# Decode attention over a long cache: larger K and V chunks, softmax by quarter heads, and a deeper add tree for the scores

## The chip, the cores and the metric

The kernel runs on one core of a Trainium2 chip. The metric is device time in microseconds from the first to the last instruction of the core. A core has a matrix engine (TensorE, PE in the profile), a vector engine (VectorE, DVE), an engine for activation functions (ScalarE, ACT), a general one (GpSimd, POOL) and one that mostly issues transfers (SyncE, SP). Data come from the off-chip memory into the on-chip SBUF, 128 partitions wide, through 16 DMA engines that all issuing engines share.

## The reference

One token is decoded. A single row `x` of 512 numbers goes through two branches, mixed by a scalar gate:

```
q = x @ wq                                  # 32 heads of 128
scores[h, k] = q[h] . K[h, k] / sqrt(128)    # K cache: 32 x 65536 x 128, bf16
o[h] = softmax(scores[h]) @ V[h]             # V cache: the same shape
a = o @ wo
b = (silu(x @ w_gate) * (x @ w_up)) @ w_down # hidden width 1792
g = sigmoid(sum(x * gate_w))
out = g * a + (1 - g) * b
```

The two caches are 537 MB each, and every byte is used once. All weights together are about 14 MB.

## The kernel before, in words

The start loads `x`, the gate's row and all weights (`wq_sb`, `wo_sb`, `wg_sb`, `wu_sb`, `wd_sb`), each whole, into one pool that stays open. TensorE makes q, already copied to all 128 partitions (`X_bc` holds x copied along columns, L67 and L85), ScalarE puts it into `q_bc_sb` (L92). The FFN branch gives `b_sb` (L96 to L134), the gate gives `gval`.

Then comes the stream, a loop over 32 heads. For each head, 16 chunks of 4096 keys are loaded, a chunk being a tile `K_t` of 128 partitions x 32 keys x 128 numbers, 1 MB, 8 KB a partition. The scores come from VectorE, not from TensorE: it multiplies the tile by q, repeated for each of the 32 keys (L175), and sums the 128 products of a key. Two adds fold them from 128 to 64 (L176) and to 32 (L180), in place; a reduce sums the last 32 (L184) into 32 columns of the head's score tile `S_sb`.

When the 512 columns of a head are there, ScalarE takes the exponential of all of them in one instruction (L189), which also leaves the sum of each row in `rowsum`. No maximum is subtracted. The result `P_sb` goes to TensorE: for each of the 16 chunks of V (`V_t`, 1 MB), 32 matmuls with 128 x 128 of V as the weights and one column of `P_sb` as the moving data, all added up in column h of `O_ps` (L203).

After the last head, the row sums are added over the partitions (L212), `O_ps` is divided by them (L214, L216), `wo` is applied (L220) and the two branches are mixed (L229, L231).

K is loaded through SP's queue, V through ACT's. There are three buffers for K, three for V, two for the products (`prod`), two for `S_sb` and two for `P_sb`. The order of the instructions on each engine isn't the order of the source: the framework picks it when it builds the program, among what it takes to be ready, and adds all waits. In the trace, for instance, the four VectorE operations of two neighbouring chunks are interleaved, and the first three V loads of a head stand ahead of its exponential. An engine carries out its own list strictly in order, so an instruction or a load that waits holds up all that stands behind it on its engine.

Of the kernel before, what the change touches and what calls it, by code (L numbers as in the profile page):

```python
# [7 lines left out]
ACT = mybir.ActivationFunctionType  # L8
ALU = mybir.AluOpType
AXIS = mybir.AxisListType  # L10
P = 128


@with_exitstack
def kernel(
# [14 lines left out]
    nc = tc.nc  # L30
    bf16 = mybir.dt.bfloat16
    f32 = mybir.dt.float32

    _, H, Sk, Dh = A_k_cache.shape
    D = A_x.shape[2]
    F = B_w_gate.shape[1]
    KT = D // P
    FT = F // P
    assert Dh == P
    W = min(4096, Sk)  # L40
    assert Sk % W == 0
    NCH = Sk // W
    J = W // P
    NB = Sk // P
    assert NB <= 512
    assert H % 4 == 0
    scale = float(Dh) ** -0.5

    consts = ctx.enter_context(tc.tile_pool(name="consts", bufs=1))
    wpool = ctx.enter_context(tc.tile_pool(name="weights", bufs=1))  # L50
    psum_q = ctx.enter_context(tc.tile_pool(name="psum_q", bufs=2, space=bass.MemoryType.PSUM))
    psum_o = ctx.enter_context(tc.tile_pool(name="psum_o", bufs=1, space=bass.MemoryType.PSUM))
    psum_misc = ctx.enter_context(tc.tile_pool(name="psum_misc", bufs=2, space=bass.MemoryType.PSUM))

    ones = consts.tile([P, P], f32, name="ones")
    nc.gpsimd.memset(ones, 1.0)

    xT = consts.tile([P, KT], bf16, name="xT")
    nc.sync.dma_start(out=xT, in_=A_x[0, 0, :].rearrange("(t p) -> p t", p=P))
    x_row = consts.tile([1, D], bf16, name="x_row")  # L60
    nc.sync.dma_start(out=x_row, in_=A_x[0])
    gw_row = consts.tile([1, D], bf16, name="gw_row")
    nc.sync.dma_start(out=gw_row, in_=gate_w.unsqueeze(0))

    X_bc = consts.tile([P, KT, P], bf16, name="X_bc")
    for t in range(KT):
        nc.vector.tensor_copy(out=X_bc[:, t, :], in_=xT[:, t : t + 1].to_broadcast([P, P]))  # L67

    wq_sb = wpool.tile([P, KT, H * Dh], bf16, name="wq_sb")
    nc.sync.dma_start(out=wq_sb, in_=A_wq.rearrange("(t p) f -> p t f", p=P))  # L70
    wo_sb = wpool.tile([P, H, D], bf16, name="wo_sb")
    nc.gpsimd.dma_start(out=wo_sb, in_=A_wo.rearrange("(h p) n -> p h n", p=P))
    wg_sb = wpool.tile([P, KT, F], bf16, name="wg_sb")
    nc.scalar.dma_start(out=wg_sb, in_=B_w_gate.rearrange("(t p) f -> p t f", p=P))
    wu_sb = wpool.tile([P, KT, F], bf16, name="wu_sb")
    nc.scalar.dma_start(out=wu_sb, in_=B_w_up.rearrange("(t p) f -> p t f", p=P))
    wd_sb = wpool.tile([P, FT, D], bf16, name="wd_sb")
    nc.gpsimd.dma_start(out=wd_sb, in_=B_w_down.rearrange("(t p) n -> p t n", p=P))

    q_bc_sb = consts.tile([P, H * Dh], bf16, name="q_bc_sb")  # L80
    HG = 4
    for g in range(H // HG):
        qg_ps = psum_q.tile([P, HG * Dh], f32, name="qg_ps")
        for t in range(KT):
            nc.tensor.matmul(  # L85
                qg_ps,
                lhsT=X_bc[:, t, :],
                rhs=wq_sb[:, t, g * HG * Dh : (g + 1) * HG * Dh],
                start=(t == 0),
                stop=(t == KT - 1),  # L90
            )
        nc.scalar.activation(  # L92
            out=q_bc_sb[:, g * HG * Dh : (g + 1) * HG * Dh], in_=qg_ps, func=ACT.Copy
        )

    gu_ps = psum_misc.tile([P, 2 * FT], f32, name="gu_ps", tag="misc")  # L96
    for ft in range(FT):
        for t in range(KT):
            nc.tensor.matmul(  # L99
                gu_ps[:, ft : ft + 1],  # L100
                lhsT=wg_sb[:, t, ft * P : (ft + 1) * P],
                rhs=xT[:, t : t + 1],
                start=(t == 0),
                stop=(t == KT - 1),
            )
        for t in range(KT):
            nc.tensor.matmul(  # L107
                gu_ps[:, FT + ft : FT + ft + 1],
                lhsT=wu_sb[:, t, ft * P : (ft + 1) * P],
                rhs=xT[:, t : t + 1],  # L110
                start=(t == 0),
                stop=(t == KT - 1),
            )
    gu_sb = consts.tile([P, 2 * FT], f32, name="gu_sb")
    nc.vector.tensor_copy(out=gu_sb, in_=gu_ps)  # L115
    eg = consts.tile([P, FT], f32, name="eg")
    nc.scalar.activation(out=eg, in_=gu_sb[:, :FT], func=ACT.Exp, scale=-1.0)
    nc.vector.tensor_scalar_add(eg, eg, 1.0)
    nc.vector.reciprocal(eg, eg)
    hprod = consts.tile([P, FT], f32, name="hprod")  # L120
    nc.vector.tensor_tensor(out=hprod, in0=gu_sb[:, :FT], in1=eg, op=ALU.mult)
    hT = consts.tile([P, FT], bf16, name="hT")
    nc.vector.tensor_tensor(out=hT, in0=hprod, in1=gu_sb[:, FT:], op=ALU.mult)
    b_ps = psum_misc.tile([1, D], f32, name="b_ps", tag="misc")
    for ft in range(FT):
        nc.tensor.matmul(  # L126
            b_ps,
            lhsT=hT[:, ft : ft + 1],
            rhs=wd_sb[:, ft, :],
            start=(ft == 0),  # L130
            stop=(ft == FT - 1),
        )
    b_sb = consts.tile([1, D], f32, name="b_sb")
    nc.vector.tensor_copy(out=b_sb, in_=b_ps)  # L134

    xg = consts.tile([1, D], f32, name="xg")
    s_t = consts.tile([1, 1], f32, name="s_t")
    nc.vector.tensor_tensor_reduce(
        out=xg, in0=x_row, in1=gw_row, scale=1.0, scalar=0.0,
        op0=ALU.mult, op1=ALU.add, accum_out=s_t,  # L140
    )
    eg2 = consts.tile([1, 1], f32, name="eg2")
    nc.scalar.activation(out=eg2, in_=s_t, func=ACT.Exp, scale=-1.0)
    nc.vector.tensor_scalar_add(eg2, eg2, 1.0)
    gval = consts.tile([1, 1], f32, name="gval")
    nc.vector.reciprocal(gval, eg2)

    kpool = ctx.enter_context(tc.tile_pool(name="kt", bufs=3))
    vpool = ctx.enter_context(tc.tile_pool(name="vt", bufs=3))
    prodpool = ctx.enter_context(tc.tile_pool(name="prod", bufs=2))  # L150
    spool = ctx.enter_context(tc.tile_pool(name="s_sb", bufs=2))
    ppool = ctx.enter_context(tc.tile_pool(name="p_sb", bufs=2))

    rowsum = consts.tile([P, H], f32, name="rowsum")
    nc.vector.memset(rowsum, 0.0)
    O_ps = psum_o.tile([P, H], f32, name="O_ps")

    for h in range(H):
        S_sb = spool.tile([P, NB], f32, name="S_sb")
        qb = q_bc_sb[:, h * Dh : (h + 1) * Dh]  # L160
        q_rep = bass.AP(
            tensor=qb.tensor,
            offset=qb.offset,
            ap=[list(qb.ap[0]), [0, J], [1, Dh]],
        )
        for c in range(NCH):
            K_t = kpool.tile([P, J, Dh], bf16, name="K_t")
            nc.sync.dma_start(
                out=K_t,
                in_=A_k_cache[0, h, c * W : (c + 1) * W, :].rearrange(  # L170
                    "(p j) d -> p j d", j=J
                ),
            )
            prod = prodpool.tile([P, J, Dh], bf16, name="prod")
            nc.vector.tensor_tensor(out=prod, in0=K_t, in1=q_rep, op=ALU.mult)  # L175
            nc.vector.tensor_tensor(  # L176
                out=prod[:, :, 0:64], in0=prod[:, :, 0:64], in1=prod[:, :, 64:128],
                op=ALU.add,
            )
            nc.vector.tensor_tensor(  # L180
                out=prod[:, :, 0:32], in0=prod[:, :, 0:32], in1=prod[:, :, 32:64],
                op=ALU.add,
            )
            nc.vector.tensor_reduce(  # L184
                out=S_sb[:, c * J : (c + 1) * J], in_=prod[:, :, 0:32],
                axis=AXIS.X, op=ALU.add,
            )
        P_sb = ppool.tile([P, NB], bf16, name="P_sb")
        nc.scalar.activation(  # L189
            out=P_sb, in_=S_sb, func=ACT.Exp, scale=scale,  # L190
            accum_out=rowsum[:, h : h + 1],
        )
        for c in range(NCH):
            V_t = vpool.tile([P, J, Dh], bf16, name="V_t")
            nc.scalar.dma_start(
                out=V_t,
                in_=A_v_cache[0, h, c * W : (c + 1) * W, :].rearrange(
                    "(p j) d -> p j d", j=J
                ),
            )  # L200
            for j in range(J):
                col = c * J + j
                nc.tensor.matmul(  # L203
                    O_ps[:, h : h + 1],
                    lhsT=V_t[:, j, :],
                    rhs=P_sb[:, col : col + 1],
                    start=(col == 0),
                    stop=(col == NB - 1),
                )

    tot_ps = psum_misc.tile([P, H], f32, name="tot_ps", tag="misc")
    nc.tensor.matmul(tot_ps, lhsT=ones, rhs=rowsum, start=True, stop=True)  # L212
    recip = consts.tile([P, H], f32, name="recip")
    nc.vector.reciprocal(out=recip, in_=tot_ps)  # L214
    oT = consts.tile([P, H], bf16, name="oT")
    nc.vector.tensor_tensor(out=oT, in0=O_ps, in1=recip, op=ALU.mult)  # L216

# [1 line left out]
    for h in range(H):  # L219
# [4 lines left out]
            start=(h == 0),  # L224
# [41 lines left out]
```

The softmax here doesn't subtract the row's maximum and nothing guards it: scores larger than these inputs give would overflow.

## Time and profile before

| | before |
|---|---|
| time, median of 4 runs | 2842.59 us (2840.87 to 2846.31) |
| span of the profiled run | 2842.2 us |
| VectorE busy | 2604.9 us, 92% |
| TensorE matmul / ScalarE busy | 535.7 us, 19% / 29.6 us, 1% |
| moved by DMA | 1090.12 MB, mean 384 GB/s |
| K_t, V_t: from issue to landing | 11.0 us, 13.8 us (median) |

The profile's page lists busy times by engine, the span in 40 slices (each digit the busy share in tenths), and the groups of instructions by source line. A row of a group reads: line, engine, operation, what is written and read with its shape, the count; then total busy time and the mean of one in ns; then how long the engine stood idle just before these instructions and what ended that. The time from issue to landing of a transfer has the transfers ahead of it in it. Rows of busy time by stretch list busy time and count of PE, PE's weight loads, DVE, ACT and POOL, then the granted clock of TensorE, the share of time that the 16 DMA engines were busy, and GB/s.

### The profile page before, as it was taken

The page shows a single profiled execution, that of the slowest core. Times are in us where ns is not written, and L with a number is a line of the kernel's source. Part 1 is how long each engine was busy: PE and PEld are TensorE (multiplying, and loading weights), DVE is VectorE, ACT ScalarE, POOL GpSimd, SP SyncE. Part 2 cuts the span into 40 slices and gives each one's busy share as a digit, 9 for nine tenths or more (in the row PEclk, how much of TensorE's full clock was granted, in tenths as well). Part 3 has the DMA queues.
Part 4 walks back from the last instruction along what each step waited for, and adds up shares of the span by engine and source line. Part 5 has one row for each costly group of instructions (what it writes and reads, how often), then busy time and mean ns, then how long its engine had stood idle before and what let it go on. Part 6 is the DMA issues. An engine that isn't in the chain of part 4 may idle for free.

```text
span 2842.2 us, 37968 instructions
## 1 busy us (share of the span) xinstructions
PE 535.7 (19%) x16576; PEld 485.7 (17%) x16576; DVE 2604.9 (92%) x2067; ACT 29.6 (1%) x75; POOL 3.3 (0%) x7
## 2 busy tenths in 40 slices
PE   2021111121111121111121111121111121111123
PEld 1021111121111121111121111121111121111122
DVE  1999999999999999999999999999999999999992
ACT  0000000000000000000000000000000000000000
POOL 0000000000000000000000000000000000000000
PEclk8555555555555555555555555555555555555555
DMA  8599999999999999999999999999999999999996
GB/s 314 198 393 388 390 390 389 416 394 391 389 390 389 415 395 387 386 389 390 416 394 391 389 387 388 416 395 387 391 388 390 415 394 390 389 389 389 417 395 235
DMA packets 151244, 1090.12 MB, mean 384 GB/s; under 512 B 16995, under 2 KB 16998, under 8 KB 19494
## 3 DMA queue, kind: packets, MB, share of 16 engines
q1 hardware_dynamic: 74790, 541.10, 46.4%
q10 hardware_dynamic: 74784, 540.57, 46.3%
q0 software_dynamic: 1504, 6.03, 0.5%
q8 instruction: 129, 2.11, 0.3%
q14 instruction: 37, 0.30, 0.0%
HBM read 1087.64 MB, written 0.00 MB: 383 GB/s over the span
## 4 chain that ended last, share of the span: by engine, by line
DVE 62%; DMA 26%; issue 10%; PE 2%; another core or an unknown queue 1%; ACT 0%; DVEq 0%; ACTq 0%; SPq 0%
DVE prod L175 30%; DMA K_t<-in_A_k_cache_dram 17%; DVE prod L176 17%; DVE prod L180 8%; DVE S_sb L184 7%; DMA V_t<-in_A_v_cache_dram 7%; DMA wu_sb<-in_B_w_up_dram 1%; PE O_ps L203 1%; PE qg_ps L85 0%; PE a_ps L220 0%; PE b_ps L126 0%; PE gu_ps L107 0%; ACT P_sb L189 0%; PE gu_ps L99 0%
## 5 line engine op out<-in xcount | busy, mean ns | idle before, releaser
L175 DVE TENSOR_TENSOR prod<-K_t,q_bc_sb 128x4096 bf16<-128x4096 bf16 x512 | 1154.4, 2286 | 125.4 <-DMA K_t<-in_A_k_cache_dram 123.6
L203 PE MATMUL O_ps<-P_sb,V_t 128*128 128x1 bf16 x16384 | 507.7, 166 | 2249.5 <-DMA V_t<-in_A_v_cache_dram 1535.0
L203 PEld LDWEIGHTS <-V_t 128*128 128x128 bf16 x16384 | 474.2, 104 | 2283.5 <-DMA V_t<-in_A_v_cache_dram 1694.3
L176 DVE TENSOR_TENSOR prod<-prod 128x2048 bf16<-128x2048 bf16 x512 | 603.1, 1220 | 0.0
L184 DVE TENSOR_REDUCE S_sb<-prod 128x32 f32<-128x1024 bf16 x512 | 599.3, 1213 | 0.0
L180 DVE TENSOR_TENSOR prod<-prod 128x1024 bf16<-128x1024 bf16 x512 | 330.0, 687 | 0.0
L189 ACT ACTIVATE P_sb<-S_sb 128x512 bf16<-128x512 f32 x32 | 20.2, 630 | 2693.3 <-DVE S_sb L184 1763.9
L216 DVE TENSOR_TENSOR oT<-O_ps,recip 128x32 bf16<-128x32 f32 x1 | 0.2, 192 | 37.7 <-PE O_ps L203 37.7
L115 DVE COPY gu_sb<-gu_ps 128x28 f32<-128x28 f32 x1 | 0.2, 186 | 31.0 <-PE gu_ps L107 31.0
L134 DVE COPY b_sb<-b_ps 1x512 f32<-1x512 f32 x1 | 0.7, 679 | 20.8 <-PE b_ps L126 20.8
L85 PE MATMUL qg_ps<-wq_sb,X_bc 128*128 128x512 bf16 x32 | 10.2, 491 | 0.0
L126 PE MATMUL b_ps<-wd_sb,hT 128*1 128x512 bf16 x14 | 5.7, 573 | 16.8 <-DMA wd_sb<-in_B_w_down_dram 16.8
L220 PE MATMUL a_ps<-wo_sb,oT 128*1 128x512 bf16 x32 | 8.6, 436 | 0.3 <-DVE oT L216 0.3
L229 DVE TENSOR_TENSOR diff<-a_ps,b_sb 1x512 f32<-1x512 f32 x1 | 0.7, 679 | 8.7 <-PE a_ps L220 8.7
L107 PE MATMUL gu_ps<-xT,wu_sb 128*128 128x1 bf16 x56 | 3.0, 165 | 20.1 <-DMA wu_sb<-in_B_w_up_dram 20.1
L99 PE MATMUL gu_ps<-xT,wg_sb 128*128 128x1 bf16 x56 | 3.1, 165 | 16.3 <-DMA wg_sb<-in_B_w_gate_dram 16.3
L67 DVE COPY X_bc<-xT 128x128 bf16<-128x128 bf16 x4 | 0.6, 222 | 5.9 <-DMA xT<-in_A_x_dram 5.9
L107 PEld LDWEIGHTS <-wu_sb 128*128 128x128 bf16 x56 | 2.6, 104 | 20.2 <-DMA wu_sb<-in_B_w_up_dram 20.2
L189 ACT ACTIVATION_READ_ACCUMULATOR P_sb<-S_sb 128x1 f32 x32 | 6.0, 187 | 0.0
L99 PEld LDWEIGHTS <-wg_sb 128*128 128x128 bf16 x56 | 2.6, 104 | 16.3 <-DMA wg_sb<-in_B_w_gate_dram 16.3
L92 ACT ACTIVATE q_bc_sb<-qg_ps 128x512 bf16<-128x512 f32 x8 | 4.8, 597 | 27.1 <-PE qg_ps L85 27.1
L126 PEld LDWEIGHTS <-hT 128*1 128x1 bf16 x14 | 1.5, 110 | 20.5 <-issue 20.4
(25 smaller groups left out, 15.9 us busy)
## 6 DMA issues: line engine op xcount, KB each, us to landing
K_t<-in_A_k_cache_dram SPq DMA_DIRECT2D x512, 1024.0 KB, 11.0
V_t<-in_A_v_cache_dram ACTq DMA_DIRECT2D x512, 1024.0 KB, 13.8
wo_sb<-in_A_wo_dram POOLq DMA_DIRECT2D x1, 4096.0 KB, 49.6
wq_sb<-in_A_wq_dram SPq DMA_DIRECT2D x1, 4096.0 KB, 26.0
wg_sb<-in_B_w_gate_dram ACTq DMA_DIRECT2D x1, 1792.0 KB, 15.5
wu_sb<-in_B_w_up_dram ACTq DMA_DIRECT2D x1, 1792.0 KB, 35.4
wd_sb<-in_B_w_down_dram POOLq DMA_DIRECT2D x1, 1792.0 KB, 59.2
xT<-in_A_x_dram SPq DMA_DIRECT2D x1, 1.0 KB, 6.1
```

What stands on the lines that cost most here:

```text
L85: nc.tensor.matmul(qg_ps, lhsT=X_bc[:, t, :], rhs=wq_sb[:, t, g * HG * Dh : (g + 1) * HG * Dh], start=(t == 0), stop=(t == KT - 1),)
L92: nc.scalar.activation(out=q_bc_sb[:, g * HG * Dh : (g + 1) * HG * Dh], in_=qg_ps, func=ACT.Copy)
L99: nc.tensor.matmul(gu_ps[:, ft : ft + 1], lhsT=wg_sb[:, t, ft * P : (ft + 1) * P], rhs=xT[:, t : t + 1], start=(t == 0), stop=(t == KT - 1),)
L107: nc.tensor.matmul(gu_ps[:, FT + ft : FT + ft + 1], lhsT=wu_sb[:, t, ft * P : (ft + 1) * P], rhs=xT[:, t : t + 1], start=(t == 0), stop=(t ...
L126: nc.tensor.matmul(b_ps, lhsT=hT[:, ft : ft + 1], rhs=wd_sb[:, ft, :], start=(ft == 0), stop=(ft == FT - 1),)
L175: nc.vector.tensor_tensor(out=prod, in0=K_t, in1=q_rep, op=ALU.mult)
L176: nc.vector.tensor_tensor(out=prod[:, :, 0:64], in0=prod[:, :, 0:64], in1=prod[:, :, 64:128], op=ALU.add,)
L180: nc.vector.tensor_tensor(out=prod[:, :, 0:32], in0=prod[:, :, 0:32], in1=prod[:, :, 32:64], op=ALU.add,)
L184: nc.vector.tensor_reduce(out=S_sb[:, c * J : (c + 1) * J], in_=prod[:, :, 0:32], axis=AXIS.X, op=ALU.add,)
L189: nc.scalar.activation(out=P_sb, in_=S_sb, func=ACT.Exp, scale=scale, accum_out=rowsum[:, h : h + 1],)
L203: nc.tensor.matmul(O_ps[:, h : h + 1], lhsT=V_t[:, j, :], rhs=P_sb[:, col : col + 1], start=(col == 0), stop=(col == NB - 1),)
L220: nc.tensor.matmul(a_ps, lhsT=oT[:, h : h + 1], rhs=wo_sb[:, h, :], start=(h == 0), stop=(h == H - 1),)
```

## The change

The change touches the stream and the start. Its aims are to give VectorE less to do for each key, to let V follow K more closely, and to get q sooner.

- A chunk is 8192 keys: tiles of 2 MB, 16 KB a partition, three for K (`KT_BUFS`) and four for V (`VT_BUFS`). VectorE works on a chunk in two halves, each as large as a chunk of before.
- In each half the add tree goes on: 128 to 64, 32, 16 and 8 by adds; the reduce sums only the last 8.
- The softmax is taken by segments of two chunks (`CHUNKS_PER_SEG` is 2), a quarter of a head: `S_sb` and `P_sb` have 128 columns and three buffers each, `rowsum` has a column for each segment, and a small reduce (`tot_h`) adds the four of a head at the end.
- At the start, `wq` is loaded in four parts on two queues, in a pool that is closed once q is made; the FFN weights are in a pool that is closed once `b_sb` and the gate are made. The K and V pools are opened after that. The load of `wo` is made to wait for q, by a one-column write into its tile.

The core of the diff:

```diff
-    W = min(4096, Sk)
+    W = min(8192, Sk)
     J = W // P
+    JH = J // 2
...
+    CPS = min(CHUNKS_PER_SEG, NCH)
+    NSEG = NCH // CPS
+    SEGCOLS = CPS * J
...
-    wq_sb = wpool.tile([P, KT, H * Dh], bf16, name="wq_sb")
-    nc.sync.dma_start(out=wq_sb, in_=A_wq.rearrange("(t p) f -> p t f", p=P))
-    nc.gpsimd.dma_start(out=wo_sb, in_=A_wo.rearrange("(h p) n -> p h n", p=P))
...
+    with tc.tile_pool(name="wq_pool", bufs=1) as wq_pool, tc.tile_pool(
+        name="psum_q", bufs=2, space=bass.MemoryType.PSUM
+    ) as psum_q:
+        wq_sb = wq_pool.tile([P, KT, H * Dh], bf16, name="wq_sb")
+        FQ = H * Dh // 4
+        for i in range(4):
+            (nc.sync if i % 2 == 0 else nc.scalar).dma_start(
+                out=wq_sb[:, :, i * FQ : (i + 1) * FQ], in_=wq_v[:, :, i * FQ : (i + 1) * FQ]
+            )
...
+    with tc.tile_pool(name="ffn_w", bufs=1) as wpool:
+        nc.gpsimd.dma_start(out=wg_sb, in_=B_w_gate.rearrange("(t p) f -> p t f", p=P))
+        nc.sync.dma_start(out=wu_sb, in_=B_w_up.rearrange("(t p) f -> p t f", p=P))
+        nc.sync.dma_start(out=wd_sb, in_=B_w_down.rearrange("(t p) n -> p t n", p=P))
+        nc.gpsimd.tensor_copy(out=wo_sb[:, 0, 0:1], in_=q_bc_sb[:, H * Dh - 1 : H * Dh])
+        nc.gpsimd.dma_start(out=wo_sb, in_=A_wo.rearrange("(h p) n -> p h n", p=P))
...
-    kpool = ctx.enter_context(tc.tile_pool(name="kt", bufs=3))
-    vpool = ctx.enter_context(tc.tile_pool(name="vt", bufs=3))
+    kpool = ctx.enter_context(tc.tile_pool(name="kt", bufs=KT_BUFS))
+    vpool = ctx.enter_context(tc.tile_pool(name="vt", bufs=VT_BUFS))
...
-            nc.vector.tensor_tensor(out=prod, in0=K_t, in1=q_rep, op=ALU.mult)
-            nc.vector.tensor_tensor(
-                out=prod[:, :, 0:64], in0=prod[:, :, 0:64], in1=prod[:, :, 64:128],
-                op=ALU.add,
-            )
-            nc.vector.tensor_tensor(
-                out=prod[:, :, 0:32], in0=prod[:, :, 0:32], in1=prod[:, :, 32:64],
-                op=ALU.add,
-            )
-            nc.vector.tensor_reduce(
-                out=S_sb[:, c * J : (c + 1) * J], in_=prod[:, :, 0:32],
-                axis=AXIS.X, op=ALU.add,
-            )
+                for u in range(2):
+                    prod = prodpool.tile([P, JH, Dh], bf16, name="prod")
+                    nc.vector.tensor_tensor(
+                        out=prod, in0=K_t[:, u * JH : (u + 1) * JH, :], in1=q_rep, op=ALU.mult
+                    )
+                    half = Dh
+                    while half > 8:
+                        half //= 2
+                        nc.vector.tensor_tensor(
+                            out=prod[:, :, 0:half], in0=prod[:, :, 0:half],
+                            in1=prod[:, :, half : 2 * half], op=ALU.add,
+                        )
+                    nc.vector.tensor_reduce(
+                        out=S_sb[:, ci * J + u * JH : ci * J + (u + 1) * JH], in_=prod[:, :, 0:8],
+                        axis=AXIS.X, op=ALU.add,
+                    )
```

For each segment of a head, after its chunks of K, the exponential of its 128 columns follows, then the two chunks of V with 64 matmuls each, adding to the same column of `O_ps` over the whole head.

## The prediction

> **What bounds the kernel now.** I read first the page's busy shares and its 40 slices, to see which resources are near full.
>
> ```profile
> PE 535.7 (19%) x16576; PEld 485.7 (17%) x16576; DVE 2604.9 (92%) x2067; ACT 29.6 (1%) x75; POOL 3.3 (0%) x7
> DVE  1999999999999999999999999999999999999992
> DMA  8599999999999999999999999999999999999996
> ```
>
> Two are nearly full at once: VectorE at 92% and the DMA engines in the nines. TensorE and ScalarE are far from any limit. The three lower digits of the DMA row matter too: slice 2 and the last are low, so there is a start and an end in which the transfers don't run full.
>
> Second, the groups by line, for what VectorE does and what it waits for:
>
> ```profile
> L175 DVE TENSOR_TENSOR prod<-K_t,q_bc_sb 128x4096 bf16<-128x4096 bf16 x512 | 1154.4, 2286 | 125.4 <-DMA K_t<-in_A_k_cache_dram 123.6
> L176 DVE TENSOR_TENSOR prod<-prod 128x2048 bf16<-128x2048 bf16 x512 | 603.1, 1220 | 0.0
> L184 DVE TENSOR_REDUCE S_sb<-prod 128x32 f32<-128x1024 bf16 x512 | 599.3, 1213 | 0.0
> L180 DVE TENSOR_TENSOR prod<-prod 128x1024 bf16<-128x1024 bf16 x512 | 330.0, 687 | 0.0
> ```
>
> All but a few us of VectorE is these four; it waits 123.6 us for K, nowhere else in the stream. Third, the timeline of VectorE in the steady part:
>
> ```profile
> 1027.26 4.49 DVE L175 TENSOR_TENSOR prod<-K_t,q_bc_sb 128x4096 bf16<-128x4096 bf16 x2
> 1031.66 2.36 DVE L176 TENSOR_TENSOR prod<-prod 128x2048 bf16<-128x2048 bf16 x2
> 1033.93 1.29 DVE L180 TENSOR_TENSOR prod<-prod 128x1024 bf16<-128x1024 bf16 x2
> 1035.14 2.34 DVE L184 TENSOR_REDUCE S_sb<-prod 128x32 f32<-128x1024 bf16 x2
> 1037.39 4.49 DVE L175 TENSOR_TENSOR prod<-K_t,q_bc_sb 128x4096 bf16<-128x4096 bf16 x2
> ```
>
> Two chunks go side by side: each operation is issued for the one, then for the other. A pair takes 1037.39 - 1027.26 = 10.13 us, so 5.065 us for 4096 keys, although the four durations sum to 2286 + 1220 + 687 + 1213 = 5406 ns: successive instructions overlap by 341/4 = 85 ns each. A head is 8 pairs, 81.0 us.
>
> Fourth, busy time by stretch, for what the DMA does inside a head:
>
> ```profile
> 1008.00:1072.00 64.00, 12.15 (x384) 11.28 (x385) 59.67 (x48) 0.00 (x0) 0.00 (x0) 0.50 1.01 422
> 1072.00:1088.00 16.00, 2.70 (x96) 2.61 (x95) 16.00 (x13) 0.72 (x2) 0.00 (x0) 0.50 0.72 267
> 68.00:147.00 79.00, 5.44 (x68) 2.91 (x67) 74.85 (x60) 3.11 (x6) 0.00 (x0) 0.54 0.48 186
> 147.10:232.30 85.20, 15.77 (x514) 14.72 (x512) 81.13 (x65) 0.72 (x2) 0.00 (x0) 0.50 0.96 395
> 2788.00:2830.00 42.00, 16.33 (x514) 15.13 (x513) 0.55 (x2) 0.46 (x2) 0.00 (x0) 0.50 0.84 326
> ```
>
> The last two columns are DMA share and GB/s. While V and K both stream, the DMA is saturated at 422 GB/s (first row); then the three V buffers are full, V must wait for the softmax of the whole head, and the rate falls to 267 (second). So a head is 85.2 us at 395 GB/s: 81.1 of VectorE and 4 of waiting for K in the saturated part. In the first head V can't run at all (186 GB/s, 79 us), and after the last K chunk V of the last head still has to come (42 us with VectorE idle). The waits confirm that end:
>
> ```profile
> DVE prod L175 <- DMA K_t<-in_A_k_cache_dram: 123.6, 51, 4.2
> DVE oT L216 <- PE O_ps L203: 37.7, 1, 37.7
> ```
>
> The bound today is thus VectorE, with the DMA 2% behind it: 33.55 MB per head at 422 GB/s is 79.5 us.
>
> **What the Trainium skill says.** "VectorE: DVE Perf Modes", The perf-mode tier table: a bf16 tensor_tensor runs two elements a cycle, a tensor_reduce one. The trace agrees: 1024 more output elements cost the add 1220 - 687 = 533 ns (0.52 ns each), and the reduce takes 1213 ns for 1024. The same page, "The DRAIN you can't avoid", has the next operation start only when the pipe is empty; here the trace differs, with 85 ns of overlap when the neighbours are independent. "DMA: Bandwidth & Descriptors", Where 436 GB/s comes from, puts a core's ceiling at 435 GB/s; I see 422. The same page, Issuing engines are not separate DMA queues: loads of SP and ACT share 16 DMA engines; the trace agrees, K and V sharing the 422.
>
> **The change part by part.**
>
> *Deeper tree (half 64, 32, 16, 8; then a reduce over 8).* Multiply and the first two adds keep their sizes, since a half chunk is again 32x128. From 1220 and 687 the add costs 154 + 0.52 n ns, so the one with 512 outputs costs 420 and that with 256 costs 287. The reduce goes from 1024 to 256 elements: at 1.04 ns an element its fixed part is 1213 - 1067 = 146, so 413. Sum per 4096 keys: 2286 + 1220 + 687 + 420 + 287 + 413 = 5313, less 6 x 85 = 4803 ns, against 5065. No trace shows adds with rows of 16 or 8; the rows of 64 and 32 cost the same per element, so I take no penalty. Upper bound: both at one element a cycle, 687 and 420, which gives 5203 ns. Over 512 units: 2459 us (upper 2664) against 2593 before.
>
> *Chunks of 8192 keys.* Loads of 2 MB, half as many. The bytes are the same; both halves of a K tile free it 4.4 us after it is begun. With 3 K and 4 V buffers, 14 MB can be in flight or waiting, against 6.
>
> *Segments of two chunks (128 exp instructions instead of 32).* Exp is between 215 ns (14 columns, L117) and 630 (512), plus 187; ScalarE is 1% busy and this hides. What it moves is V: TensorE may use V after a quarter head, and four V buffers hold two segments. On ACT, the V loads wait for a V buffer and the next exp is queued behind them; but the buffer is freed by TensorE within about 4 us of an exp (32 matmuls take 1.0 us; 128 make 4), and the next exp is 19 us off, so nobody waits for that. In steady state a segment needs 4 x 2.097 MB = 8.39 MB, 19.9 us at 422, while VectorE needs 4 x 4.80 = 19.2. The DMA becomes the bound, and K being always short keeps it full.
>
> *First head and end.* V lags K by a segment and not a head, so the 79 us at 186 GB/s and the 42 us at the end mostly go. At the end after the last K chunk: two units 9.6, exp 0.8, 128 matmuls 4, and what now follows the last V matmul (2829.8 to 2842.2) 12.4: 27 us; 30 with some backlog on VectorE.
>
> *Start.* wq in four loads, wo held until q exists, FFN weights in a pool that is closed before the K pool opens. If K tiles reuse this memory (32 + 42 KB a partition), the first K load waits for the FFN matmuls; behind it on SP are all K loads, and VectorE waits for these. Estimate: wq (4.2 MB, 10 us at 422 GB/s, and about 2 to begin) by 12 us; 32 q matmuls at 0.38 (16 took 6.03 us) to about 26; FFN weights (5.5 MB, 13 us alone, more beside wo and V) to 45; the FFN's matmuls (3 us for the first two products) and the first K tile (2 MB, 5 to 10 us) to 57. Before, the stream began at 42 and stood still from 51 to 72 for b_sb, which is much the same. Meanwhile wo and four V tiles (8.4 MB) can load. I put 15 us of idle DMA here (0 to 35). The four more output columns of tot and tot_h at the end cost below 1 us.
>
> *Sum.* Bytes as before, 1090 MB, at 422 GB/s: 2583 us; first bytes 3; idle at the start 15; end 30: **2631 us**. The other side: VectorE would be through at 57 + 2459 + 17 = 2533, so it waits about 100 us for K.
>
> **Rivals.**
> - *The DMA runs faster with 16 KB rows.* For: half as many descriptors. Against: 422 is already near a share of 1.01, and 435 is the stated ceiling. At 430: 2535 + 48 = 2583 us.
> - *The DMA keeps its gaps* (share 0.96 as in today's heads, for K and V filling together). For: 395 GB/s in each head. Against: today's gap comes from VectorE being slower than the DMA and from the wait of a whole head. 1090/0.405 + 48 = 2739 us.
> - *Short rows run at half rate*, and VectorE stays the bound: 57 + 2664 + 17 = 2738 us.
> - *The halves aren't interleaved.* Then every instruction follows the one it depends on. In the FFN chain at 40.2 us such neighbours have a gap of 0.04 us in place of the overlap: 5313 + 6 x 40 = 5553 ns, 2843 in all, and 57 + 2843 + 17 = 2917 us, slower. For: two halves of one tile are new. Against: two prod buffers, as today, where the order came out interleaved.
>
> **How the numbers follow.** Forecast 0.62; faster DMA 0.10; gaps 0.12; short rows 0.08; no interleaving 0.07; about the same through a mix of losses 0.01. The predicted time is 2631. From 2580 to 2740 takes in the first four, with the ends of start (0 to 35 us) and rate, and leaves out some of the short rows and the slower one. Faster 0.92, same 0.01, slower 0.07.
>
> **What would show it.** Right: DMA at 0.97 or more in nearly every slice at about 420 GB/s; the two new adds near 420 and 287 ns, the reduce near 413; pairs of units at 9.6 us when K is there; a wait for K near 100 us; K wait as the largest item of the chain; oT waiting 6 us or less behind TensorE's last stretch. Wrong: VectorE above 97% busy in the middle (short rows), single instructions with gaps between them (no interleaving), or slices at 390 GB/s with both K and V full.

## The result, and the profile after

The changed kernel takes 2613.55 us (median of 8 runs, 2612.91 to 2615.25). Its ratio to the kernel before is 0.9195, 95% interval [0.9186, 0.9204]. The forecast was 2631 us; it was 17 us too long, for a gain of 229 us where 212 were forecast.

From the page of the changed kernel, the busy shares and the slices:

```profile
PE 482.6 (18%) x16576; PEld 467.1 (18%) x16576; DVE 2485.0 (95%) x3093; ACT 58.1 (2%) x267; POOL 3.2 (0%) x8
DVE  0899999999999999999999999999999999999997
DMA  9999999999999999999999999999999999999995
GB/s 342 370 425 427 427 426 428 427 427 427 427 427 427 427 427 427 428 427 427 427 426 425 425 426 423 427 425 425 427 424 427 424 426 426 425 426 425 424 426 216
```

The same row of the kernel before:

```profile
GB/s 314 198 393 388 390 390 389 416 394 391 389 390 389 415 395 387 386 389 390 416 394 391 389 387 388 416 395 387 391 388 390 415 394 390 389 389 389 417 395 235
```

The GB/s rows decide. In all slices but the first two and the last the rate now stands at 423 to 428, where before it stood at 386 to 417. VectorE's share has risen to 95%, though its work has shrunk: the span has shrunk more. That high share is a trap, and the experiments show it.

The groups of VectorE's stream, different shapes kept apart (mean ns of one after the comma):

```profile
L200 DVE TENSOR_TENSOR prod<-K_t,q_bc_sb 128x4096 bf16<-128x4096 bf16 x512 | 1150.0, 2288 | 45.3 <-DMA K_t<-in_A_k_cache_dram 30.0 <-DVE S_sb L210 0.9
L206 DVE TENSOR_TENSOR prod<-prod 128x2048 bf16<-128x2048 bf16 x512 | 602.7, 1219 | 0.0
L206 DVE TENSOR_TENSOR prod<-prod 128x1024 bf16<-128x1024 bf16 x512 | 329.5, 685 | 0.0
L206 DVE TENSOR_TENSOR prod<-prod 128x512 bf16<-128x512 bf16 x512 | 193.3, 419 | 0.0
L210 DVE TENSOR_REDUCE S_sb<-prod 128x32 f32<-128x256 bf16 x512 | 189.1, 411 | 0.3 <-DVE prod L206 0.3
L206 DVE TENSOR_TENSOR prod<-prod 128x256 bf16<-128x256 bf16 x512 | 124.8, 285 | 0.0
```

The three new sizes cost 419, 285 and 411 ns. The timeline of VectorE at the start of the stream shows how they are strung:

```profile
67.68 0.68 DVE L156 COPY b_sb<-b_ps 1x512 f32<-1x512 f32 x1 [16.31 <-PE b_ps L149]
75.33 4.49 DVE L200 TENSOR_TENSOR prod<-K_t,q_bc_sb 128x4096 bf16<-128x4096 bf16 x2 [6.97 <-DMA K_t<-in_A_k_cache_dram]
79.74 4.63 DVE L206 TENSOR_TENSOR prod<-prod 128x2048 bf16<-128x2048 bf16 x8
84.29 0.74 DVE L210 TENSOR_REDUCE S_sb<-prod 128x32 f32<-128x256 bf16 x2
84.95 4.48 DVE L200 TENSOR_TENSOR prod<-K_t,q_bc_sb 128x4096 bf16<-128x4096 bf16 x2
```

The two halves of a chunk go in step: two multiplies, eight adds, two reduces. Where K is there, a pair takes 84.95 - 75.33 = 9.62 us. Over the whole stream it is slower: the last pair ends at 2592.9 us, and (2592.9 - 75.3)/256 is 9.83 us. The excess is 256 x 0.21 = 55 us in all. The group of the multiply shows 45.3 us of idle time ahead of it; 7.0 of these lie ahead of the first pair, so 38 us belong to the excess, mostly behind K and in gaps of a few tenths of a us. The other 17 us I put down to overlap between neighbours that is lost where a multiply has to wait; no view shows that by itself. With K in plenty (half of V loaded, below) the excess is gone.

Busy time by stretch (the last two columns are DMA share and GB/s) gives the balance of the transfers:

```profile
0.00:90.00 90.00, 18.45 (x158) 8.43 (x159) 18.08 (x30) 6.48 (x11) 3.19 (x8) 0.68 0.88 341
90.00:150.00 60.00, 10.65 (x384) 10.47 (x384) 60.00 (x76) 1.21 (x6) 0.00 (x0) 0.50 0.97 397
900.00:1200.00 300.00, 53.28 (x1920) 53.63 (x1921) 294.22 (x369) 6.14 (x30) 0.00 (x0) 0.50 1.01 427
2560.00:2612.00 52.00, 16.63 (x290) 10.51 (x290) 35.25 (x51) 0.80 (x4) 0.00 (x0) 0.59 0.38 160
```

The page counts 1090.1 MB, which at about 426.5 GB/s, the rate of the stream, are 2556 us. What a stretch moves less than that rate is called lost DMA time here. In the first 90 us 30.7 MB were moved, 72 us worth: 18 us lost. In the next 60, 4 us lost. In the last 52, 8.3 MB or 20 us worth: 32 us lost. The sum, 2556 + 18 + 4 + 32 = 2610 us, is within 2 us of the span of 2611.8. Lost isn't always idle: from 30 to 60 us, while the weights load, the DMA share is 1.03 at only 376 GB/s, and that is 4 of the 18 us.

### The profile page after: what moved, and what is told of

The parts are those of the page before. It is cut to its first block, busy times and chain, and to the rows that moved or that the text cites. A ratio compares the mean times of both kernels' runs of the same rounds, so it can differ in the third digit from the quotient of the medians.

```text
span 2611.8 us, 38109 instructions
## 1 busy us (share of the span) xinstructions
PE 482.6 (18%) x16576; PEld 467.1 (18%) x16576; DVE 2485.0 (95%) x3093; ACT 58.1 (2%) x267; POOL 3.2 (0%) x8
## 2 busy tenths in 40 slices
DMA packets 80189, 1090.10 MB, mean 417 GB/s; under 512 B 8851, under 2 KB 10646, under 8 KB 14486
## 4 chain that ended last, share of the span: by engine, by line
DVE 50%; DMA 48%; PE 1%; issue 1%; DVEq 0%; SPq 0%; ACT 0%; ACTq 0%
DMA K_t<-in_A_k_cache_dram 46%; DVE prod L200 28%; DVE prod L206 20%; DVE S_sb L210 3%; DMA wd_sb<-in_B_w_down_dram 1%; DMA wq_sb<-in_A_wq_dram 1%; PE a_ps L258 0%; PE b_ps L149 0%; PE qg_ps L96 0%; PE O_ps L231 0%; DVEq L200 0%; DVE out_sb L269 0%; DVE diff L267 0%; PE tot_ps L240 0%; SPq L69 0%
## 5 line engine op out<-in xcount | busy, mean ns | idle before, releaser
L200 DVE TENSOR_TENSOR prod<-K_t,q_bc_sb 128x4096 bf16<-128x4096 bf16 x512 | 1150.0, 2288 | 45.3 <-DMA K_t<-in_A_k_cache_dram 30.0
L206 DVE TENSOR_TENSOR prod<-prod 128x2048 bf16<-128x2048 bf16 (+3 forms) x2048 | 1186.0, 652 | 0.0
L231 PE MATMUL O_ps<-P_sb,V_t 128*128 128x1 bf16 x16384 | 454.6, 165 | 2074.8 <-ACT P_sb L215 2074.8
L231 PEld LDWEIGHTS <-V_t 128*128 128x128 bf16 x16384 | 455.4, 104 | 2074.4 <-issue 1688.3
L210 DVE TENSOR_REDUCE S_sb<-prod 128x32 f32<-128x256 bf16 x512 | 189.1, 411 | 0.3 <-DVE prod L206 0.3
L215 ACT ACTIVATE P_sb<-S_sb 128x128 bf16<-128x128 f32 x128 | 39.6, 309 | 2491.4 <-DVE S_sb L210 2412.3
L215 ACT ACTIVATION_READ_ACCUMULATOR P_sb<-S_sb 128x1 f32 x128 | 23.9, 186 | 0.0
L149 PE MATMUL b_ps<-wd_sb,hT 128*1 128x512 bf16 x14 | 5.2, 553 | 12.4 <-DMA wd_sb<-in_B_w_down_dram 12.4
## 6 DMA issues: line engine op xcount, KB each, us to landing
K_t<-in_A_k_cache_dram SPq DMA_DIRECT2D x256, 2048.0 KB, 24.8
```

The lines of the kernel that those rows point to most:

```text
L149: nc.tensor.matmul(b_ps, lhsT=hT[:, ft : ft + 1], rhs=wd_sb[:, ft, :], start=(ft == 0), stop=(ft == FT - 1),)
L200: nc.vector.tensor_tensor(out=prod, in0=K_t[:, u * JH : (u + 1) * JH, :], in1=q_rep, op=ALU.mult)
L206: nc.vector.tensor_tensor(out=prod[:, :, 0:half], in0=prod[:, :, 0:half], in1=prod[:, :, half : 2 * half], op=ALU.add,)
L210: nc.vector.tensor_reduce(out=S_sb[:, ci * J + u * JH : ci * J + (u + 1) * JH], in_=prod[:, :, 0:8], axis=AXIS.X, op=ALU.add,)
L215: nc.scalar.activation(out=P_sb, in_=S_sb, func=ACT.Exp, scale=scale, accum_out=rowsum[:, h * NSEG + sgi : h * NSEG + sgi + 1],)
L231: nc.tensor.matmul(O_ps[:, h : h + 1], lhsT=V_t[:, j, :], rhs=P_sb[:, col : col + 1], start=(gcol == 0), stop=(gcol == NB - 1),)
```

## The experiments

Two theories were to be told apart. **A**: the DMA bounds the changed kernel; its time is bytes over rate, plus the time lost at the start and the end. **B**: VectorE, 95% busy, still bounds it. Three further questions were what each part of the change brings, why the rate rose from 422 to 427 GB/s, and whether the time lost at start and end can be had back. The ratios are to the kernel before as it was run beside each kernel.

| kernel | time, us | ratio to before, 95% interval |
|---|---|---|
| changed kernel | 2613.55 | 0.9195 [0.9186, 0.9204] |
| shallow tree in it | 2690.81 | 0.9462 [0.9446, 0.9478] |
| three adds left out | 2608.25 | 0.9174 [0.9158, 0.9189] |
| half of V loaded | 2550.19 (one run) | |
| tree alone, in the kernel before | 2752.39 | 0.9681 [0.9667, 0.9696] |
| softmax of a whole head | 2635.72 | 0.9269 [0.9255, 0.9283] |
| 8 KB rows, 1 MB transfers | 2645.64 | 0.9302 [0.9288, 0.9316] |
| two runs of 8 KB, 2 MB transfers | 2650.63 | 0.9325 [0.9309, 0.9341] |
| K pool first | 2591.68 | 0.9112 [0.9099, 0.9126] |
| K pool first, wo early | 2590.61 | 0.9109 [0.9095, 0.9123] |
| K pool first, wo a quarter head earlier | 2587.56 | 0.9101 [0.9088, 0.9115] |

### Which engine is the bound

Take work off VectorE:

```diff
-                    while half > 8:
+                    while half > 64:
```

> The changed kernel without the adds to 32, 16 and 8: the reduce sums the first 8 of the 64 partial products, so most of each score is left out. VectorE has 1.14 us less for each 4096 keys, 583 us in all; bytes, buffers and order stay. Theory A (DMA bound): only the last two units show it, 2 to 8 us: about 2608 us, VectorE near 1900 us busy. Theory B (VectorE bound or as good as): below 2580 us.

2608.25 us. VectorE's busy time fell from 2485 us to 1904.7, and the time by 5.3 us. The page's groups show where the rest went:

```profile
L200 DVE TENSOR_TENSOR prod<-K_t,q_bc_sb 128x4096 bf16<-128x4096 bf16 x512 | 1150.2, 2288 | 619.9 <-DMA K_t<-in_A_k_cache_dram 619.9
```

All of it but these 5 us became waiting for K. B would have needed a large drop. Then take bytes off the DMA:

```diff
-                    out=V_t,
+                    out=V_t[:, :JH, :],
...
-                    )
+                    )[:, :JH, :]
...
-                        lhsT=V_t[:, j, :],
+                        lhsT=V_t[:, j % JH, :],
```

> The changed kernel with only the first half of each V tile loaded and used twice (half of V is left out of the computation); VectorE, TensorE and K stay as they are. 268 MB less are moved. Theory A: the DMA is no longer the bound, and the time falls to what VectorE needs: 75 + 256 pairs x 9.61 + 19 = 2554 us, with VectorE waiting for K nowhere after the start. Theory B: VectorE is the bound already, so 2612 us.

2550.19 us, and in the middle of the stream VectorE never stops while the DMA runs at 330 GB/s:

```profile
900.00:1200.00 300.00, 53.25 (x1920) 52.34 (x1920) 300.00 (x375) 6.14 (x30) 0.00 (x0) 0.50 0.87 330
```

With the same VectorE work and fewer bytes the time falls by 63 us, to VectorE's own bound (2554 us by the sum of the expectation). So both runs say A, and this one says how far the second bound lies below: 2.4%.

### What each part brings

The old tree in the changed kernel:

```diff
-                    while half > 8:
+                    while half > 32:
...
-                        out=S_sb[:, ci * J + u * JH : ci * J + (u + 1) * JH], in_=prod[:, :, 0:8],
+                        out=S_sb[:, ci * J + u * JH : ci * J + (u + 1) * JH], in_=prod[:, :, 0:32],
```

> The changed kernel with the old tree (adds to 32, then a reduce over 32); all else stays. If the changed kernel is bound by the DMA (theory A), its own VectorE bound lies below it and this edit makes VectorE the bound again: stream from 75 us, 512 x 5.065 = 2593 us, 18 us after: 2687 us, DMA share falling to about 0.96. If VectorE is still the bound in the changed kernel (theory B), the whole difference of 512 x 0.26 = 134 us shows: 2746 us.

2690.81 us, 4 us from the forecast of A. VectorE is busy for all of the 300 us from 900 on, and its waits for K come to 7.1 us on the whole page:

```profile
900.00:1200.00 300.00, 53.32 (x1920) 52.40 (x1920) 300.00 (x239) 6.14 (x30) 0.00 (x0) 0.50 1.00 415
```

The deeper tree is thus worth 77 us here, of the 134 us that it takes off VectorE; the DMA stops the rest. The DMA share was forecast to fall to 0.96 and didn't: it reads 1.00 at 415 GB/s, though VectorE is the bound here.

The new tree alone, in the kernel before:

```diff
-            nc.vector.tensor_tensor(
-                out=prod[:, :, 0:64], in0=prod[:, :, 0:64], in1=prod[:, :, 64:128],
...
+            half = Dh
+            while half > 8:
+                half //= 2
+                nc.vector.tensor_tensor(
...
-                out=S_sb[:, c * J : (c + 1) * J], in_=prod[:, :, 0:32],
+                out=S_sb[:, c * J : (c + 1) * J], in_=prod[:, :, 0:8],
```

> The kernel before with nothing but the deeper tree (adds to 8, reduce over 8). VectorE then needs 512 x 0.26 = 134 us less. If the rest of the change (segments, chunks, buffers) is what lets VectorE's saving through (theory A), the DMA's floor of 79.5 us a head plus its pause while V is full, about 2 us, stops it: 31 heads of 81.5 us in place of 85.2, 4 us less in the first head: about 2725 us. If the tree alone brings its whole saving (rival), 2708 us or less; if the DMA is already the bound of each head (other rival), 2835 us.

2752.39 us: the tree alone brings 91 us, where the forecasts of 2725 and 2708 meant 118 and 135. From one exponential to the next a head takes (2699.15 - 224.46)/30 = 82.5 us, where it took 85.25 before and 81.5 were expected. Stretches of the trace within one head show what the tree can't reach:

```profile
1032.00:1036.00 4.00, 0.00 (x0) 0.10 (x1) 2.94 (x8) 0.00 (x0) 0.00 (x0) 0.50 1.02 426
1044.00:1048.00 4.00, 0.00 (x0) 0.00 (x0) 4.00 (x8) 0.00 (x0) 0.00 (x0) 0.50 0.93 387
1048.00:1052.00 4.00, 1.78 (x67) 1.78 (x67) 4.00 (x4) 0.72 (x2) 0.00 (x0) 0.50 0.53 182
```

While V streams, VectorE stands for part of the time (2.94 of 4 us busy) because the DMA is full; just before the exponential, V's three buffers are full and the rate drops to 182 GB/s. Each of the two waits for the other in turn. The two runs together: the tree brings 91 us alone, everything else brings 153 alone, and both bring 229, somewhat less than the sum, as is to be expected where the DMA sets a floor.

The lag of V behind K, with the softmax of a whole head again:

```diff
-CHUNKS_PER_SEG = 2
+CHUNKS_PER_SEG = 8
```

> The changed kernel with the softmax of a whole head at once (CHUNKS_PER_SEG 8), all else as changed. V then lags K by a head as before. Theory A: the first head runs with K alone after V's four buffers are full (VectorE bound, 77 us at about 218 GB/s, some 35 us of DMA time lost), and at the end four chunks of V (8.4 MB, 20 us) come after the last exponential: 2614 + 35 + 16 = 2665 us, with heads in the middle still near 79 us. If the finer segments are not what fills start and end, 2614 us.

2635.72 us: the direction is right, the size is 22 us and not 51. The start, the middle and the end of this run:

```profile
90.00:150.00 60.00, 0.00 (x0) 0.00 (x0) 60.00 (x76) 0.00 (x0) 0.00 (x0) 0.50 0.60 216
600.00:1200.00 600.00, 112.40 (x3904) 108.85 (x3904) 588.70 (x732) 5.79 (x16) 0.00 (x0) 0.50 1.01 427
2580.00:2633.00 53.00, 23.62 (x546) 17.34 (x545) 13.95 (x25) 0.72 (x2) 0.00 (x0) 0.59 0.53 220
```

In the first head K runs alone at 216 GB/s. Against the changed kernel's 397 that is 11 MB less by 150 us, or 25 us of DMA time, and 3 more by 180 us. My forecast had 35 for it. The four V tiles that come after the last exponential aren't lost time at all: in the last 53 us the DMA still moves 11.7 MB, so that 26 us are lost, against 32 in the changed kernel. The forecast had added 16 us for this end. The sum, 28 - 6, is the 22 us.

The middle has no gap at 427 GB/s, as expected here, though V again waits for a whole head. So the quarter heads bring their 22 us at the start; the gaps within the heads, which the tree alone leaves open, are closed by something else in the change. What is left is the larger chunks and the memory of the buffers, 14 MB against 6. The run with chunks of 4096 keys and 14 MB of buffers, below, has no gaps either, which points to the memory; no run changed it alone.

### Where the rate comes from

Chunks of 4096 keys, with twice the buffers:

```diff
-    W = min(8192, Sk)
+    W = min(4096, Sk)
-    JH = J // 2
+    JH = J
...
-KT_BUFS = 3
-VT_BUFS = 4
-CHUNKS_PER_SEG = 2
+KT_BUFS = 6
+VT_BUFS = 8
+CHUNKS_PER_SEG = 4
...
-                for u in range(2):
+                for u in range(1):
```

> The changed kernel with chunks of 4096 keys (1 MB transfers, 8 KB a partition), with 6 K and 8 V buffers, segments of 4 chunks and no halves: same memory, same segments, same VectorE work. If the 426 GB/s of the changed kernel come from the longer rows, the rate goes back to 422 and the time to about 2640 us. If they come from having more bytes in flight, it stays at 426 and 2614 us. Two tiles are needed for a pair here, not two halves of one; that should change nothing.

2645.64 us, at 421 GB/s from 900 to 1200 us. Row length and transfer size both changed here, so a second run kept the transfers of 2 MB and cut only the rows:

```diff
-                    out=K_t,
+                    out=K_t.rearrange("p (a j) d -> p a j d", a=2),
...
-                        "(p j) d -> p j d", j=J
+                        "(a p j) d -> p a j d", a=2, j=JH
```

V is loaded in the same way.

> The changed kernel with the same 2 MB transfers, buffers and halves, but each partition takes two runs of 8 KB (one for each half of a tile) and not one of 16 KB. It tells row length from transfer size, which the run with 8 KB rows changed together. If the length of a run sets the rate, it is 420 GB/s and the time 2645 us, as in that run; if the number and size of transfers does, 426 GB/s and 2614 us. VectorE's work is the same in either case.

2650.63 us. The GB/s row of its page, against the one of the changed kernel above:

```profile
GB/s 337 374 420 421 420 421 421 421 421 421 421 421 421 421 420 421 421 420 421 421 421 418 421 419 418 421 418 419 417 421 419 418 421 417 420 420 419 418 420 215
```

Same transfers, same buffers, same VectorE work, 421 in place of 427. So it is the length of the contiguous run in DRAM, for each partition, that makes the difference; the size and number of the transfers don't show in the rate. Nor does the order of the addresses: here a transfer reads two blocks side by side, in the run before it reads one, and both give 421. The 5 us between these two runs lie in the last slice (215 GB/s here, 246 there). The cost can be estimated: 131072 runs of 8 KB became 65536 of 16 KB (the page counts 145725 packets here and 80189 in the changed kernel), which is 4096 fewer on each of 16 DMA engines, and 37.1 us less: 9 ns a run.

### Start and end

The K pool opened ahead of the pools for the weights, so that K's tiles don't wait for the FFN's memory:

```diff
+    kpool = ctx.enter_context(tc.tile_pool(name="kt", bufs=KT_BUFS))
+
     with tc.tile_pool(name="wq_pool", bufs=1) as wq_pool, tc.tile_pool(
...
-    kpool = ctx.enter_context(tc.tile_pool(name="kt", bufs=KT_BUFS))
```

> The changed kernel with the K pool opened ahead of the pools of the weights, so that no K tile takes their memory (V's tiles do). The stream can then begin at about 25 us, when q is there, and not at 75 us. Theory A (bytes over rate, with about 20 us of idle DMA in the first 90 us): only that idle time can go, so 2595 us. Theory B (VectorE bound): the stream begins 50 us earlier and ends 50 us earlier, 2565 us. If the start doesn't matter at all, 2614 us.

2591.68 us. The same stretches as above:

```profile
0.00:90.00 90.00, 21.58 (x286) 11.94 (x286) 52.42 (x76) 7.28 (x15) 4.62 (x8) 0.67 0.98 387
90.00:150.00 60.00, 11.19 (x384) 10.70 (x384) 60.00 (x74) 1.21 (x6) 0.00 (x0) 0.50 1.01 427
2540.00:2590.00 50.00, 20.04 (x411) 13.77 (x408) 31.52 (x42) 0.80 (x4) 0.00 (x0) 0.59 0.49 204
```

34.8 MB by 90 us, which leaves 8 us lost in place of 18; none from 90 to 150 in place of 4; and at the end 10.2 MB, or 24 us worth, in 50 us: 26 us lost in place of 32. Together 20 of the 22 us; why the end gains 6 was not looked into. VectorE's first K operation came at 20.5 us and not at 75.3. It then stood still for `b_sb`, but the third pair still began at 59.8 us and not at 94.6, 35 us sooner, and the end came only 22 sooner: again A. So opening K's pool behind those of the weights costs the changed kernel 22 us. q is complete at 24.8 us, where it took until 72.0 before, but K then waits for memory until 67.67. What the new start brings against the old one was not run by itself.

Last, the work after the last V matmul. In the changed kernel 32 matmuls of wo (8.9 us) stand there. For the next two runs, `rowsum` and `O_ps` are split into 31 heads and the last one, and the first 31 are divided and multiplied by wo within the last head:

```diff
+            if h == H1 and sgi == NSEG - 1:
+                finish(rowsum1, O1_ps, H1, 0)
```

> The K pool opened first, as in the run before, and the end shortened: the first 31 heads are divided by their sums and go through wo while the last quarter of the last head is still being loaded, so that after the last V matmul only one head is left (one matmul of wo for 32, which took 8.9 us). Expected 2592 - 9 = 2583 us. If the 32 matmuls were hidden at the end already, 2592 us; if the early division makes VectorE wait for TensorE in the last quarter, more than 2592.

2590.61 us, no gain over 2591.68. The timeline of TensorE and ScalarE tells why:

```profile
2570.22 9.62 PE L198 MATMUL a_ps<-wo_sb,oT 128*1 128x512 bf16 x31
...
2574.32 0.31 ACT L245 ACTIVATE P_sb<-S_sb 128x128 bf16<-128x128 f32 x1 [17.86 <-DVE S_sb L240]
...
2579.77 3.38 PE L261 MATMUL O_ps<-P_sb,V_t 128*128 128x1 bf16 x128
```

The 31 matmuls came between the V matmuls of the last two quarters, and the last exponential was done at 2574.6 while they ran until 2579.8. They no longer stand at the end, but the last V matmuls start only behind them, 5 us after their exponential. So once more, a quarter head sooner:

```diff
-            if h == H1 and sgi == NSEG - 1:
+            if h == H1 and sgi == NSEG - 2:
```

> As the run with wo early, but the division of the first 31 heads and their wo matmuls are placed one quarter head earlier, so that the 31 matmuls (9.6 us on TensorE, in order) are through before the last quarter's V is needed. The last V matmul should then end with V's landing, as with the K pool first alone (2575.7 us), and 8 us follow in place of 14: 2584 us. If TensorE's matmuls still stand ahead of V's last ones, 2590 us.

2587.56 us, 4 us less than with the K pool first alone, of 8 expected. The wo matmuls now end at 2565, and the last V matmul at 2580.3 is set by V's landing, but that V lands later than the 2575.7 us of the run without the split. What moved it was not settled: VectorE's order in this last part is less regular with the split. This is the fastest version: 0.9101 of the time before, and 1% under the changed kernel.

## Why the prediction was right, step by step

**The bound before and after.** The step that VectorE bounds each head with the DMA 2% behind, and that the deeper tree turns this round, held. The runs with less VectorE work and with fewer bytes show it on both sides. The latter, at 2550 us, also bears out the other side of the sum: 2533 us for VectorE, and 18 more because K began later. The rival that the DMA keeps its gaps fell with the GB/s row; its 405 GB/s are what the tree alone gives (405 to 407 in the middle of that run). My reason against it was right only in part: I put the gaps down to VectorE and to the wait of a whole head, and the run with whole heads has no gaps in the middle.

**The price of the tree.** Forecast 420, 287 and 413 ns, found 419, 285 and 411; a pair of units at 9.61 us, found 9.62. The line through the two adds with rows of 64 and 32 held for rows of 16 and 8: the rival of short rows fell. The two halves came out interleaved, so the slower rival fell too.

**Segments.** No wait arose behind V's loads on ACT: all 128 exponentials began within 0.4 us of the end of the last reduce before them. V's four buffers let it run ahead: before its V matmuls TensorE stood idle for 2074.8 us, and the profile puts all of it down to the exponential. After the last one only 128 matmuls remained (3.55 us; 4 were forecast).

**The start.** The first K load was to wait for the FFN's memory, and did: it was issued at 67.67 us, right behind the last FFN matmul. The chain and the waits of SP's queue show what held it:

```profile
24.64 37.71 DMA wd_sb<-in_B_w_down_dram
SPq L192 <- PE b_ps L149: 5.3, 1, 5.3
```

VectorE began on K at 75.3 us and not at 57. I had put the landing of all FFN weights at 45 us; two of them were there by 47, but `wd_sb`, issued at 24.64, took 37.71 us and landed at 62.4. Then came the third product, 5.2 us, which I had left out. What counts for the time is the lost DMA time, and there 3 + 15 were forecast and 18 + 4 found. That these lie so close is in part luck: the 15 was put, not worked out, and the start that it belongs to was 18 us off.

**The end.** 30 us forecast, 32 found. The last pair took 9.7 us, exponential and matmuls 4.1, and what follows the last V matmul 14.8, where 9.6, 4.8 and 12.4 were forecast. That leaves 3 us for VectorE's backlog, as was put.

**The rate** is the term that was mis-sized. I took 422 GB/s, so 2583 us for the bytes; it was 426.5, so 2556 us. That is 27 us too many, and 4 too few at the start and 2 at the end made up for part of it. The rival of a faster DMA was right in its cause, longer rows, and too high in its size (430). My argument against it, that a share of 1.01 leaves no room, was wrong: the run with 8 KB rows shows a share of 1.01 at 421 GB/s, the one with 16 KB 1.01 at 427. The share doesn't measure the room that is left: it also reads 1.00 at 415 GB/s in the shallow tree, where VectorE is the bound, and 0.87 with half of V, at 330 GB/s, which is 77% of 427.

**The wait for K** was forecast near 100 us and is 55 with the lost overlap (38 of idle time). With K starting 18 us later and the DMA 27 us faster, the same sum gives about 55. Of the chain that ended last, 46% is the DMA of K, the largest item, as forecast.

## What to carry to other kernels

When two resources are nearly full, work out for each stage what each alone would need, and forecast from the larger; a saving on one is worth only the distance to the other (here 77 us of 134). A busy share of 95% doesn't name the bound, and a DMA share of 1.00 doesn't either: take work off that engine and see if the time moves. In a kernel that the DMA bounds, count bytes over the rate that a saturated stretch shows, and then look for lost DMA time at the start (memory that is handed on late) and at the end.

## What the runs showed of the hardware

At the same transfer size, contiguous runs of 16 KB for each partition moved at 427 GB/s on this core and runs of 8 KB at 421. By the difference in time each run more costs some 9 ns on its DMA engine (an estimate, 37.1 us over 4096 runs). The DMA share of the profile doesn't tell the two apart: it reads 1.01 in both. A tensor_tensor of bf16 costs no more for each result with short rows: 419 ns for 512 results in rows of 16 and 285 ns for 256 in rows of 8, where the line through the longer rows gives 420 and 287.
